# Sparse attention and two expert layers on one core: the first batch's attention in two halves of 288 tokens, and another order of the last products

## The chip, the cores and the metric

The kernel runs on one core of a Trainium2 chip. A core has five engines that run side by side, each through its own list of instructions in order: TensorE (PE) multiplies matrices, VectorE (DVE) and ScalarE (ACT) work on elements, GpSimd (POOL) too but without access to PSUM, and SyncE (SP) issues most of the DMAs, which move data between the core's memory (SBUF) and DRAM. TensorE writes to PSUM, eight banks of 128 x 512 floats. The metric is the device time of one execution in microseconds (us); lower is better.

## The reference

Two heads of 64 channels make a pair, four pairs a batch. Pairs 0 and 1 have the local mask, pairs 2 and 3 the strided one. The output of attention, 2304 tokens of 512 channels, goes through two expert layers.

```python
batch, n_heads, seq, head_dim = (4, 8, 576, 64)      # q, k, v
stride = 32
scores = scale * np.matmul(q, k.transpose(0, 1, 3, 2))
rel = pos[:, None] - pos[None, :]
mask_local = (rel >= 0) & (rel < stride)
mask_strided = (rel >= 0) & (pos[None, :] % stride == pos[:, None] % stride)
masks = [mask_local if h < H // 2 else mask_strided for h in range(H)]
attn = softmax(np.where(masks, scores, -1e9)) @ v
x = attn.transpose(0, 2, 1, 3).reshape(2304, 512)
h = x @ w_in                                         # 512 -> 2048
x = np.where(h >= 1, h, np.where(h <= -1, 0, (h + 1) ** 2 / 4)) @ w_out
r = np.maximum(x @ w2_in, 0)
out = (s * (r * r) + b) @ w2_out
```

## The kernel before, in words

**Tiling.** Tokens come in nine blocks of N = 256 for each expert layer: block g below 9 belongs to the first layer, g from 9 to 17 to the second. The 2048 inner channels make eight parts p of 256. `layer1(g, p)` gives the inner channels of a part for a block in 24 products of 128 x 256 into one PSUM tile h; `activate` applies the function and writes g; `layer2` multiplies by the second weights into y. Each float is held as the sum of two shorter numbers (names in h and l: xh, xl), so one product of the algorithm is three on TensorE. The second layer's second product is done by seven products m1 to m7 for four quadrants (Strassen's way in Winograd's form); `combine` makes the operands and `finish_fast` adds the seven into the quadrants c11, c12, c21, c22.

**Weights.** Each of 32 weight tiles of the first layer (wr{f}_{0 or 1}, 512 KB; 0 is w_in, 1 is w_out) is loaded and then converted: ScalarE makes c, VectorE makes wc in two instructions, ScalarE the high half of w, GpSimd the low half.

**Attention.** A `Unit` is one pair of one batch: loads of q, k, v; transposes on TensorE (t); scores (s); maximum, subtraction, exponential, sum, reciprocal and multiplication on VectorE and ScalarE; transposes of the result (p); products with v (o); copies into xr, from which `x_split` makes xh and xl of a block. In the strided pairs every 32nd token makes a group, 18 tokens by 3 residues in one tile of 54. The first batch's units borrow the memory of weight tiles 4 to 15 (`borrowed`), so those weights can only be loaded once the unit has read its data for the last time. Block 0 holds tokens 0 to 255, block 1 tokens 256 to 511.

**What sets the order.** `Order` records every instruction with a time at which it is due (`nc.now`, in slots of about 2.9 us, from the tables STARTS, PACE, W_TIMES and from the loops), and `Order.issue` then walks all engines with prices for every instruction and writes out the list of each engine. In front of the first product of layer 1 it also puts idle products (`fill`) into TensorE's list where it counts on a wait, to keep that engine's clock up. On the chip nothing of this is decided again: each engine takes its list in order. The passes begin with parts 0 and 1 of block 0, then parts 0 and 1 of block 1, and layer 2 follows two steps behind (LAG).

**Lines that matter here.** All instructions are written by one line, 383, so views are read by the names of tiles. The tables are STARTS (51), MEMORY (55), PASSES (62) and W_TIMES (73); the units are at 432, `x_split` at 790, `combine` at 873, `layer2_fast` at 895, `finish_fast` at 910. The call that plans the units:

```python
for i, t in enumerate(STARTS):
    b, pair = divmod(i, 4)
    plan(Unit(b, FIRST_PAIRS[pair], borrowed(MEMORY[i]) if i in MEMORY else main, i < QUICK, i < NATURAL), t)
```

Of the kernel before, what the change touches and what calls it, by code (L numbers as in the profile page):

```python
# [12 lines left out]
F32 = mybir.dt.float32  # L13
# [29 lines left out]
PITCH = 64  # L43
RES = 3
# [3 lines left out]
)  # L48
US_PER_SLOT = 2.9

STARTS = (-14, -11.2, -13.5, -11.7, 1.8, 8, 14.7, 21.4, 31, 37, 43, 48, 58, 64, 70, 76)
# [17 lines left out]

AGAIN = (6, *range(9, 16))  # L70


W_TIMES = {0: (-7, 1.9, 3), 1: (7.9, 1.9, 2.6)}
W_NEXT = {0: (113, 1.4), 1: (150, 3.2)}
W_AHEAD, W_RETRY, W_GAP = 3, 0.5, 1.2
# [18 lines left out]
N_CONST = N_MASK_L + N_MASK_S + P  # L94
# [7 lines left out]
def constants():  # L102

    row = np.arange(P)[:, None] % 64
    col = np.arange(64)[None, :]
    back = row % 32 - (col - 32)
    local = np.where((back >= 0) & (back < STRIDE), 0, DROP).astype(np.float32)
    last = np.where(row < 32, np.where(row >= col, 0, DROP), local).astype(np.float32)
    c = np.arange(54)[None, :]
    same = ((row // NPOS == c // NPOS) & (c % NPOS <= row % NPOS)) | (row >= 54)  # L110
    strided = np.where(same, 0, DROP).astype(np.float32)
    return np.ascontiguousarray(
        np.concatenate([last, local, strided, np.eye(P, dtype=np.float32)], axis=1)
    )


class Order:
# [151 lines left out]
    def issue(self):  # L269
# [40 lines left out]
        while done < n:  # L310
# [76 lines left out]
def attention_moe_moe(ctx, tc, q, k, v, w1_in, w1_out, w2_in, w2_out, s_in, b_in, consts, out):  # L387
# [7 lines left out]
    mask_l, mask_s, ident_b = narrow[:, :N_MASK_L], narrow[:, N_MASK_L:N_MASK_L + N_MASK_S], narrow[:, N_MASK_L + N_MASK_S:]  # L395
# [15 lines left out]
    filled = [0] * B  # L411
# [13 lines left out]
    def put(b, copy, o, i):  # L425
        copy(o, i)
        filled[b] += o.partition_size() * o.free_size()
# [232 lines left out]

    rooms, half_rooms, halves = [], [], {}
# [128 lines left out]
    def x_split(g):  # L790
# [57 lines left out]
    def activate(g, p, h):  # L848
        u = nc.tile(sb, [P, 2 * N], F32, tag="u", bufs=U_BUFS, name=f"u{g}_{p}")
        gt = nc.tile(sb, [P, 2, 2 * N], F32R, tag="g", bufs=3, name=f"g{g}_{p}")  # L850
# [22 lines left out]
    def combine(g, p, u, h, gt):  # L873
# [5 lines left out]
        gl = turn(1, (*main["raw"], main["s"]), f"gl{g}_{p}")[:, :7 * P].bitcast(F32R)  # L879

        def split(x, c):
            nc.scalar.activation(out=gh[:, c], in_=x, func=AF.Copy)
            nc.gpsimd.tensor_tensor(out=gl[:, c], in0=x, in1=gh[:, c].bitcast(F32), op=ALU.subtract)
# [6 lines left out]
        split(s4, slice(3 * P, 7 * P))  # L890
# [4 lines left out]
    def layer2_fast(g, p, p0, p1):  # L895
# [4 lines left out]
        left = dict(a11=0, a22=1, a12=2, s1=3, s2=4, s3=5, s4=6)  # L900
        for n, a, b in (
            (0, "a11", "b11"), (1, "a12", "b21"), (6, "a22", "t4"), (2, "s1", "t1"), (3, "s2", "t2"), (4, "s3", "t3"), (5, "s4", "b22"),
        ):
            c = slice(left[a] * P, (left[a] + 1) * P)
# [5 lines left out]
    def finish_fast(g, p0, p1):  # L910
# [3 lines left out]
        (c21, c22), (c11, c12), (m1, m2), (m5, m6), (m7, m3), (m4, _) = [(x[:, :HM], x[:, HM:]) for x in (*o, *y)]  # L914
# [67 lines left out]
    def borrowed(i):  # L982

        def piece(n, a=0, b=2 * DM):
# [7 lines left out]
            raw=[piece(0, 0, 768), piece(1, 0, 768)], qk=[piece(2), piece(3)], s=piece(4), p=[piece(5), piece(0, 0, 384)],  # L992
            v=[piece(6), piece(7)],
# [50 lines left out]
    with tc.manual_schedule():  # L1044
        nc.now = -100
        nc.sync.dma_start(out=ident, in_=consts[:, N_MASK_L + N_MASK_S:])
# [12 lines left out]
        for i, t in enumerate(STARTS):  # L1059
            b, pair = divmod(i, 4)  # L1060
            plan(Unit(b, FIRST_PAIRS[pair], borrowed(MEMORY[i]) if i in MEMORY else main, i < QUICK, i < NATURAL), t)
# [12 lines left out]
        for n, (g, p0, p1) in enumerate(PASSES):  # L1074
# [7 lines left out]
            nxt = PASSES[n + 1][0] if n + 1 < len(PASSES) else g  # L1082
            for i, (layer, b, *pp, p) in enumerate(order):
# [7 lines left out]
                if i == p1 - p0 + 1 and nxt not in xs:  # L1091
                    x_split(nxt)
                slot += 1
        for _, b, *pp, p in behind:
            nc.now += 1
            second(b, p, *pp)
# [27 lines left out]
```

## Time and profile before

| | |
|---|---|
| three runs | 897.02 us median, 896.44 to 901.4 |
| the profiled execution | 900.46 us, its span 898.7 us |
| TensorE | busy 878.2 us (98%), mean granted clock 0.988 |
| VectorE, ScalarE, GpSimd | busy 481.0, 491.7, 422.7 us |
| DMA | 103.38 MB, 125246 packets, 86656 of them under 512 B |

The span runs from the first to the last instruction that the profiler saw. A busy share says little of one stage, since the kernel has three: a start, in which attention of the first batch and the first weights come in; a long middle, in which the products follow each other; an end, in which the last products are added up and stored. The rows further down are read stage by stage.

### The profile page before, as it was taken

To read this page: it belongs to the slowest core of one execution; us is meant where nothing else is said; L and a number is where in the kernel's file an instruction comes from. 1 tells how busy PE (TensorE), PEld (TensorE's weight loads), DVE (VectorE), ACT (ScalarE), POOL (GpSimd) and SP (SyncE) were. 2 spreads that over 40 slices of the span, in tenths; PEclk is the share of its full clock that TensorE was granted. 3 is DMA by queue.
4 is the path that set the end of the run, shared out by engine and by line. 5 is a ranking of instruction groups with operands and counts; after the bars stand their busy time and mean duration, and the time that the engine had idled before them with its cause. 6 is when DMAs were issued, how large, how long until landed. Compare 5 with 4: busy or idle time off the path is not lost.

```text
span 898.7 us, 21961 instructions
## 1 busy us (share of the span) xinstructions
PE 878.2 (98%) x8872; PEld 866.4 (96%) x8872; DVE 481.0 (54%) x993; ACT 491.7 (55%) x1097; POOL 422.7 (47%) x362
## 2 busy tenths in 40 slices
PE   8889999999999999999999999999999999999996
PEld 7879999899999999999999999999999999999996
DVE  2598554444434342333685788545458954554455
ACT  2587685444534343333554587656667655555553
POOL 6186462112212212223464578777745765455544
PEclk9889999999999999999999999999999999999998
DMA  9998233322322221002635633426135332222211
GB/s 176 317 325 251 76 89 88 76 41 53 68 50 64 53 85 48 25 24 74 214 110 193 220 130 119 154 105 211 71 100 183 120 116 94 95 95 94 94 49 48
DMA packets 125246, 103.38 MB, mean 115 GB/s; under 512 B 86656, under 2 KB 103296, under 8 KB 125144
## 3 DMA queue, kind: packets, MB, share of 16 engines
q1 hardware_dynamic: 122008, 100.78, 37.5%
q8 instruction: 70, 1.15, 0.5%
q10 hardware_dynamic: 2368, 0.59, 0.4%
q0 software_dynamic: 768, 0.60, 0.4%
q14 instruction: 32, 0.26, 0.1%
HBM read 73.63 MB, written 28.31 MB: 113 GB/s over the span
## 4 chain that ended last, share of the span: by engine, by line
PE 95%; DVE 2%; issue 1%; DMA 1%; ACT 0%; SPq 0%; POOL 0%; DVEq 0%; ACTq 0%; POOLq 0%
PE h L383 45%; PE y L383 43%; PE s L383 3%; PE o L383 2%; PE idle L383 1%; DMA wr<-in_moe_w_in_dram 1%; PE t L383 1%; PE p L383 1%; DVE o L383 1%; DVE wc L383 0%; DVE u L383 0%; ACT u L383 0%; DVE h L383 0%; ACT h L383 0%; DVE qk L383 0%
## 5 line engine op out<-in xcount | busy, mean ns | idle before, releaser
L383 PE MATMUL h<-xh,w 128*128 128x256 f32 x2304 | 435.4, 281 | 3.9 <-ACT xr L383 2.0
L383 PEld LDWEIGHTS h<-xh,w 128*128 128x128 f32 x2304 | 364.3, 189 | 5.1 <-ACT xr L383 2.1
L383 PE MATMUL h<-xl,w 128*128 128x256 f32 x1152 | 323.6, 281 | 0.5 <-DVE xl L383 0.5
L383 PE MATMUL y<-g,w 128*128 128x256 f32 x1728 | 220.4, 281 | 0.0
L383 PEld LDWEIGHTS h<-xl,w 128*128 128x128 f32 x1152 | 218.0, 189 | 1.0 <-DVE xl L383 0.8
L383 POOL TENSOR_TENSOR g<-u,g 128x512 fp32r<-128x512 f32 x72 | 95.6, 1327 | 246.7 <-ACT g L383 166.7
L383 PEld LDWEIGHTS y<-g,w 128*128 128x128 f32 x1728 | 209.0, 188 | 0.8
L383 PE MATMUL y<-w,g 128*128 128x256 f32 x864 | 158.7, 281 | 0.9 <-DVE o L383 0.9
L383 ACT ACTIVATE u<-h 128x512 f32<-128x512 f32 x144 | 85.9, 598 | 117.6 <-DVE h L383 55.8
L383 PEld LDWEIGHTS y<-w,g 128*128 128x128 f32 x864 | 132.9, 188 | 1.3 <-DVE o L383 1.3
L383 DVE TENSOR_SCALAR u<-h 128x512 f32<-128x512 f32 x72 | 49.6, 688 | 142.5 <-PE h L383 139.9
L383 PE MATMUL y<-w,gl 128*128 128x256 f32 x432 | 121.0, 282 | 0.0
L383 POOL TENSOR_TENSOR gl<-u,g 128x384 fp32r<-128x384 f32 x72 | 76.1, 1057 | 95.4 <-ACT g L383 93.5
L383 ACT ACTIVATE u<-u,half 128x512 f32<-128x512 f32 x72 | 51.9, 722 | 113.7 <-DVE u L383 113.6
L383 POOL TENSOR_TENSOR gl<-s,g 128x512 fp32r<-128x512 f32 x72 | 97.8, 1358 | 33.1 <-ACT g L383 31.2
L383 ACT ACTIVATE g<-u 128x512 fp32r<-128x512 f32 (+1 forms) x144 | 83.1, 577 | 32.1 <-DVE u L383 25.2
L383 DVE TENSOR_SCALAR h<-h,sbt 128x512 f32<-128x512 f32 x72 | 58.7, 816 | 68.1 <-ACT h L383 67.9
L383 POOL TENSOR_TENSOR w<-wc,w 128x512 fp32r<-128x512 f32 x56 | 76.6, 1375 | 37.9 <-ACT w L383 36.0
L383 PEld LDWEIGHTS y<-w,gl 128*128 128x128 f32 x432 | 80.9, 188 | 0.0
L383 DVE TENSOR_TENSOR o<-y,o 128x256 f32<-128x256 f32 x120 | 46.7, 417 | 45.3 <-PE y L383 45.1
L383 DVE TENSOR_TENSOR u<-h,u 128x512 f32<-128x512 f32 x72 | 49.5, 687 | 26.3 <-ACT u L383 25.9
L383 DVE TENSOR_SCALAR wc<-wr 128x512 int32<-128x512 int32 x64 | 45.4, 722 | 19.8 <-DMA wr<-in_moe_w_in_dram 10.6
(91 smaller groups left out, 934.5 us busy)
## 6 DMA issues: line engine op xcount, KB each, us to landing
wr<-in_moe_w_in_dram SPq DMA_DIRECT2D x32, 512.0 KB
wr<-in_moe_w_out_dram SPq DMA_DIRECT2D x32, 512.0 KB
x<-o SPq DMA_DIRECT2D x36, 256.0 KB
scratch<-x SPq DMA_DIRECT2D x18, 512.0 KB
y<-o SPq DMA_DIRECT2D x22, 256.0 KB
scratch<-y SPq DMA_DIRECT2D x11, 512.0 KB
out_dram<-o SPq DMA_DIRECT2D x18, 256.0 KB
xhd<-xh SPq DMA_DIRECT2D x8, 512.0 KB
```

The lines of the kernel that those rows point to most:

```text
L383: getattr(getattr(self.nc, engine), op)(*args, **kw)
```

## The change

Two parts, and new numbers in the tables.

1. **The first batch's units come in halves** (`Half`): tokens 0 to 287, then 288 to 575. The first halves of all four pairs stand in front of the second halves. A half loads 288 rows of q and k (the local pairs also only half of v), transposes them in one bank, has one tile of scores instead of two, and its own softmax, p, o and copies. A second half of a strided pair looks at the keys of both halves. Its k transposes and all copies of the strided pairs into xr go to VectorE instead of ScalarE. Block 0 may be split once the first halves are there.
2. **The last block's end** (`last_two`; the seven products also stand in another order, PRODUCTS, in all blocks of the second layer): the last two parts are multiplied product by product, both parts of m1, m6, m2, m5, then of m4, m7, then m3; the sums of the four quadrants are made as the products come, with GpSimd and ScalarE taking some of them; every quadrant has a DMA of its own, two on SyncE's queue and two on ScalarE's. `layer1` of the last part moves in front of the second product of the part two before, and the low half of the last two parts' s goes from GpSimd to VectorE.

```diff
+PRODUCTS = ((0, "b11"), (4, "t2"), (2, "b21"), (3, "t1"), (1, "t4"), (5, "t3"), (6, "b22"))
+HALF_PACE = (
+    (0, ("load_qk", 0)), (0, ("load_qk", 1)), (1, ("load_v",)), (3, ("trans", 0)), (3.1, ("trans", 1)), (3.6, ("scores",)),
...
-STARTS = (-14, -11.2, -13.5, -11.7, 1.8, 8, 14.7, 21.4, 31, 37, 43, 48, 58, 64, 70, 76)
+HALF_STARTS = ((-14.0, -9.0), (-13.0, -8.0), (-14.0, -8.43), (-13.5, -8.28))
+STARTS = (1.07, 7.73, 14.33, 22.7, 31, 37, 43, 48, 58, 64, 70, 76)
-W_TIMES = {0: (-7, 1.9, 3), 1: (7.9, 1.9, 2.6)}
-W_AHEAD, W_RETRY, W_GAP = 3, 0.5, 1.2
+W_TIMES = {0: (-7.02, 1.9, 3.0), 1: (8.01, 1.9, 2.6)}
+W_AHEAD = 4.25
...
-                dma = max(dma, t + 1.0) + o.nbytes() / run * (10 + 0.039 * run) / 16e3
+                dma = max(dma, t + 1.0) + o.nbytes() / run * (15 + 0.04 * run) / 16e3
...
+    class Half(Unit):
+        def __init__(self, b, pair, mem, h):
+            self.nb, self.kw = (6, 27 * (h + 1)) if self.strided else (5, 64)
...
+        def load_qk(self, w):
+            queue = nc.scalar if w and not self.h else nc.sync
+            for a in range(2):
+                queue.dma_start(
+                    out=t[:, :, 64 * a:64 * a + 64],
+                    in_=self.heads((q, k)[w])[a][HALF * self.h:HALF * (self.h + 1)].rearrange("(i s) d -> s i d", s=96),
+                )
+        def trans(self, w):
+            bk = bank(f"t{w}_{self.id}")[:, :HALF]
...
+            copy = nc.vector.tensor_copy if h and w else act_copy
...
+        def scores(self):
+            self.sp = bank(f"s_{self.id}")[:, :nb * kw]
...
+        def smul(self):
+            nc.vector.tensor_tensor(out=self.s, in0=self.s, in1=self.by(self.mx), op=ALU.mult)
...
+        def evac_o(self, copy):
+            if self.strided:
+                for g in range(2):
...
+                    put(self.b, nc.vector.tensor_copy, o, self.ob[g][:, :135].rearrange("p (m e t) -> p m e t", e=RES, t=NPH), h)
+                put(self.b, nc.vector.tensor_copy, t[:, 30:], self.ob[0][:, 135:153].rearrange("p (e t) -> p e t", t=NPH), h)
...
-                assert filled[b] == P * NC * S, (g, filled)
+                assert filled[b] == P * NC * S or hi <= HALF and ready[0] == P * NC * HALF, (g, filled)
...
-        split(s4, slice(3 * P, 7 * P))
+        split(s4, slice(3 * P, 7 * P), nc.vector if g == LAST[0] and p >= NP - 2 else nc.gpsimd)
...
+    def last_two(g, p0, part):
...
+        for i, n in ((0, 0), (0, 1), (0, 2), (0, 3), (1, 0), (1, 1), (1, 2), (1, 3), (0, 4), (0, 5), (1, 4), (1, 5), (0, 6), (1, 6)):
+            multiply(n, *pairs[i])
+        nc.scalar.activation(out=c11, in_=m1, func=AF.Copy)
+        nc.gpsimd.tensor_tensor(out=p11, in0=c11, in1=p11, **add)
+        nc.vector.tensor_tensor(out=c21, in0=m6, in1=c11, **add)
+        nc.gpsimd.tensor_tensor(out=p21, in0=c21, in1=p21, **add)
+        nc.vector.tensor_tensor(out=c22, in0=m5, in1=c21, **add)
+        nc.gpsimd.tensor_tensor(out=p22, in0=c22, in1=p22, **add)
+        nc.vector.tensor_tensor(out=c11, in0=m2, in1=p11, **add)
+        leave(1, 0, c11, nc.sync)
+        nc.vector.tensor_tensor(out=p12, in0=c22, in1=p12, **add)
+        nc.scalar.activation(out=p11, in_=m7, func=AF.Copy)
+        nc.vector.tensor_tensor(out=p21, in0=m7, in1=p21, **add)
+        nc.gpsimd.tensor_tensor(out=c22, in0=p11, in1=p22, **add)
+        leave(0, 1, c22, nc.sync)
+        nc.vector.tensor_tensor(out=c21, in0=p21, in1=m4, op=ALU.subtract)
+        leave(0, 0, c21, nc.scalar)
+        nc.vector.tensor_tensor(out=c12, in0=m3, in1=p12, **add)
+        leave(1, 1, c12, nc.scalar)
...
-        for i, t in enumerate(STARTS):
+        for i, (t0, t1) in enumerate(HALF_STARTS):
+            mem = borrowed(MEMORY[i]) if i in MEMORY else rest
+            for h, t in enumerate((t0, t1)):
+                u = Half(0, FIRST_PAIRS[i], mem, h)
+                u.clear()
+                plan(u, t)
+        for i, t in enumerate(STARTS, 4):
...
+            if n + 1 == len(PASSES):
+                order.insert(-2, order.pop(-2))
```

What that makes of the lists is shown at three places.

SyncE's queue around the first weights (mem and raw are a unit's q, k and v, named by the borrowed weight; wr0_f_x is weight tile f, x of the first layer). Before:

```order
L383 DMA mem4_0_214<-in_v_dram 128x4x64 x2
L383 DMA mem4_0_214<-in_v_dram 64x64
L383 DMA mem4_1_261<-in_v_dram 128x4x64 x2
L383 DMA mem4_1_261<-in_v_dram 64x64
L383 DMA wr0_0_0_305<-in_moe_w_in_dram 128x4x256
L383 DMA wr0_1_0_324<-in_moe_w_in_dram 128x4x256
L383 DMA wr0_0_1_351<-in_moe_w_out_dram 128x1024
L383 DMA wr0_2_0_384<-in_moe_w_in_dram 128x4x256
```

and now:

```order
L401 DMA mem4_0_136<-in_v_dram 128x2x64 x2
L401 DMA mem4_1_145<-in_v_dram 128x2x64 x2
L401 DMA raw0_0_3_161<-in_q_dram 96x3x64 x2
L401 DMA mem11_0_175<-in_q_dram 96x3x64 x2
L401 DMA wr0_0_0_200<-in_moe_w_in_dram 128x4x256
L401 DMA wr0_1_0_212<-in_moe_w_in_dram 128x4x256
L401 DMA mem15_0_84<-in_q_dram 96x3x64 x2
L401 DMA mem15_1_69<-in_k_dram 96x3x64 x2
L401 DMA mem12_0_113<-in_v_dram 128x2x64 x2
L401 DMA mem12_0_113<-in_v_dram 64x64
```

The first two weights now stand behind the loads of the first halves (16 DMAs on this queue) instead of behind all 24 of the batch; 28 of the 44 loads that there are now follow them. The third weight, wr0_0_1, stands between second halves.

TensorE around the first product of layer 1 (h0_0; o are the products with v, p the transposes in front of them, idle the products that fill). Before:

```order
L383 MATMUL o0_0_1_558<-mem7_0_99,mem4_0_214 64x32 x2
L383 MATMUL o0_0_1_558<-mem7_0_99,mem4_1_261 64x32 x2
L383 MATMUL p0_0_3_608<-ident_65,s_0_3_71 128x128 x4
L383 MATMUL idle_83<-u_67 128x256 x29
L383 MATMUL h0_0_673<-xh0_648,w0_0_0_657 128x256
L383 MATMUL h0_0_673<-xl0_661,w0_0_0_657 128x256
L383 MATMUL p0_0_2_684<-ident_65,mem9_0_73 128x128 x4
L383 MATMUL p1_0_3_691<-ident_65,s_0_3_71 128x128 x2
```

and now:

```order
L401 MATMUL o0_0_1a_447<-mem5_1_414,mem4_0_136 64x32
L401 MATMUL o0_0_1a_447<-mem5_1_414,mem4_1_145 64x32
L401 MATMUL idle_78<-u_67 128x256 x12
L401 MATMUL p_0_3a_499<-ident_65,s0_0_3_96 128x128 x3
L401 MATMUL idle_78<-u_67 128x256 x11
L401 MATMUL h0_0_530<-xh0_516,w0_0_0_505 128x256
L401 MATMUL o0_0_3a_535<-early_528,v0_0_3_106 64x27
L401 MATMUL o1_0_3a_537<-early_528,v0_0_3_106 64x27
```

The idle products stay, 23 here in two groups instead of 29 in one. Behind the first product stand instructions of both halves: five more products of h0_0 are spread over the next 42 rows of the list, and its other 18, all of h0_1's and those of h1_0 follow p_0_1b and p_0_3b, the transposes of two second halves, at row 173 and 174.

VectorE's last rows (y15_4_0 to 3 are the banks of the seven products, o the quadrants, scratch the partial sum of the earlier parts). Before:

```order
L383 TENSOR_TENSOR o15_4_0_12187<-y15_4_1_12053,o15_4_1_12176 128x256
L383 TENSOR_TENSOR o15_4_1_12176<-y15_4_0_12033,o15_4_1_12176 128x256
L383 TENSOR_TENSOR o15_4_1_12176<-y15_4_1_12053,o15_4_0_12187 128x256
L383 TENSOR_TENSOR o15_4_0_12187<-y15_4_2_12062,o15_4_0_12187 128x256
L383 TENSOR_TENSOR o15_4_1_12176<-y15_4_2_12062,o15_4_1_12176 128x256
L383 TENSOR_TENSOR o15_4_0_12187<-y15_4_1_12053,o15_4_0_12187 128x256
L383 TENSOR_TENSOR o15_4_0_12187<-o15_4_0_12187,y15_4_3_12047 128x256
L383 TENSOR_TENSOR o15_4_0_12187<-o15_4_0_12187,scratch_4754 128x512
```

and now:

```order
L401 TENSOR_TENSOR gl15_6_12270<-s15_6_12252,g15_6_12259 128x512
L401 TENSOR_TENSOR s15_7_12286<-h15_7_12195,s15_7_12286 128x128
L401 TENSOR_TENSOR last_l_12303<-s15_7_12286,last_h_12293 128x512
L401 TENSOR_TENSOR o15_4_0_12334<-y15_4_0_12231,o15_4_1_12326 128x256
L401 TENSOR_TENSOR o15_4_0_12334<-y15_4_1_12237,o15_4_0_12334 128x256
L401 TENSOR_TENSOR o15_4_1_12326<-y15_4_1_12237,scratch_4915 128x256
L401 TENSOR_TENSOR scratch_4915<-o15_4_0_12334,scratch_4915 128x256
L401 TENSOR_TENSOR scratch_4915<-y15_4_2_12241,scratch_4915 128x256
L401 TENSOR_TENSOR o15_4_1_12326<-y15_4_3_12263,scratch_4915 128x256
L401 TENSOR_TENSOR o15_4_0_12334<-scratch_4915,y15_4_2_12241 128x256
```

The wide addition of the partial sum, 128x512, is gone from the last place; the partial sum is added quadrant by quadrant on the way, and the row that reads the last product's bank, y15_4_3, is the last but one.

## Rows read from the trace of the kernel before

**Rows 1.** Windows: busy time by engine in each stretch, TensorE clock, DMA share, GB/s.

```profile
0.00:60.00 60.00, 49.18 (x714) 45.96 (x715) 32.16 (x63) 32.28 (x71) 30.29 (x41) 0.86 1.09 260
21.00:51.80 30.80, 25.32 (x407) 23.48 (x402) 19.45 (x36) 18.43 (x43) 9.43 (x7) 0.81 1.03 298
60.00:150.00 90.00, 90.00 (x1113) 87.81 (x1112) 56.17 (x97) 63.27 (x170) 51.62 (x42) 1.00 0.49 145
890.00:899.00 9.00, 1.78 (x15) 1.54 (x13) 3.82 (x8) 0.39 (x1) 1.78 (x2) 0.70 0.15 58
```

**Rows 2.** Timeline of TensorE, 30 to 64: start, length, instruction, count, idle before.

```profile
32.92 0.66 PE L383 MATMUL o<-mem,mem 64*64 64x32 f32 x30 [2.95 <-issue]
...
35.57 5.81 PE L383 MATMUL idle<-u 128*128 128x256 f32 x29
41.22 0.28 PE L383 MATMUL h<-xh,w 128*128 128x256 f32 x1
...
47.56 0.58 PE L383 MATMUL h<-xh,w 128*128 128x256 f32 x1 [2.03 <-ACT xr L383]
...
58.16 0.36 PE L383 MATMUL h<-xh,w 128*128 128x256 f32 x1 [1.62 <-DVE u L383]
...
61.07 3.00 PE L383 MATMUL y<-g,w 128*128 128x256 f32 x24
```

**Rows 3.** Timeline of SyncE's DMA queue, 0 to 30: start, time of issue, count.

```profile
1.65 2.37 SPq L383 DMA_DIRECT2D mem<-in_q_dram  x4
...
13.17 10.34 SPq L383 DMA_DIRECT2D mem<-in_v_dram  x12
23.56 1.14 SPq L383 DMA_DIRECT2D wr<-in_moe_w_in_dram  x2
```

**Rows 4.** DMA view, packets of 15 to 27, then of 27 to 31.

```profile
DMA packets 6579, 2.16 MB, mean 180 GB/s; under 512 B 6019, under 2 KB 6485, under 8 KB 6578
...
DMA packets 1132, 1.53 MB, mean 382 GB/s; under 512 B 44, under 2 KB 1001, under 8 KB 1131
```

**Rows 5.** Timelines of ScalarE, GpSimd and VectorE, 42 to 52.

```profile
42.09 0.60 ACT L383 ACTIVATE mem<-p 128x512 f32<-128x512 f32 x1 [2.27 <-PE p L383]
...
43.83 3.94 POOL L383 TENSOR_TENSOR w<-wc,w 128x512 fp32r<-128x512 f32 x3 [4.16 <-ACT w L383]
...
45.15 2.90 DVE L383 TENSOR_SCALAR wc<-wr 128x512 int32<-128x512 int32 x2 [4.21 <-DMA wr<-in_moe_w_in_dram]
...
49.41 2.36 DVE L383 TENSOR_TENSOR xl<-xr,xh 128x512 fp32r<-128x512 f32 x2
```

**Rows 6.** Groups of VectorE by form: busy, mean ns of one, idle before.

```profile
L383 DVE TENSOR_SCALAR wc<-wr 128x512 int32<-128x512 int32 x64 | 45.4, 722 | 19.8 <-DMA wr<-in_moe_w_in_dram 10.6 <-DMA wr<-in_moe_w_out_dram 4.9 <-POOL w L383 4.2
L383 DVE SCALAR_TENSOR_TENSOR wc<-c,wc 128x512 int32<-128x512 int32 x64 | 42.9, 680 | 6.9 <-ACT c L383 6.3
...
L383 DVE COPY o<-y 128x512 f32<-128x512 f32 x18 | 12.4, 688 | 4.6 <-PE y L383 4.2
...
L383 DVE TENSOR_REDUCE mx<-s 128x6 f32<-128x324 f32 x8 | 4.0, 496 | 11.6 <-PE s L383 11.3
```

**Rows 7.** The end: chain of waits, then timelines of TensorE, VectorE, SyncE's queue.

```profile
884.18 7.14 PE y L383 x59
...
891.50 0.28 PE L383 MATMUL y<-w,gl 128*128 128x256 f32 x1
...
891.40 2.41 DVE L383 TENSOR_TENSOR o<-y,o 128x256 f32<-128x256 f32 x6 [2.92 <-PE y L383]
...
894.30 1.12 DVE L383 TENSOR_TENSOR o<-o,scratch 128x512 f32<-128x512 f32 x1
...
894.90 0.88 SPq L383 DMA_DIRECT2D out_dram<-o  x2
```

**Rows 8.** Timelines of VectorE at 879 and of GpSimd at 889.

```profile
879.62 1.57 DVE L383 TENSOR_TENSOR o<-o,scratch 128x512 f32<-128x512 f32 x1
...
889.23 1.28 POOL L383 TENSOR_TENSOR gl<-s,g 128x512 fp32r<-128x512 f32 x1
```

More of the change, by code (lines that the diff above doesn't have):

```diff
@@ L111, in constants @@
     strided = np.where(same, 0, DROP).astype(np.float32)
+    at, pos = np.divmod(row % 32, NPH)
+    halves = []
+    for h in range(2):
+        n = NPH * (h + 1)
+        c = np.arange(3 * n)[None, :]
+        halves.append(np.where((at == c // n) & (c % n <= pos + NPH * h) | (at >= 3), 0, DROP).astype(np.float32))
     return np.ascontiguousarray(
-        np.concatenate([last, local, strided, np.eye(P, dtype=np.float32)], axis=1)
+        np.concatenate([last, local, strided, *halves, np.eye(P, dtype=np.float32)], axis=1)
     )
@@ L423, in x_raw, with put @@
         return xr[b]
-    def put(b, copy, o, i):
+    def put(b, copy, o, i, h=None):
         copy(o, i)
-        filled[b] += o.partition_size() * o.free_size()
+        n = o.partition_size() * o.free_size()
+        filled[b] += n
+        if h is not None:
+            ready[h] += n
     def act_copy(o, i):
@@ L849, in activate @@
         u = nc.tile(sb, [P, 2 * N], F32, tag="u", bufs=U_BUFS, name=f"u{g}_{p}")
-        gt = nc.tile(sb, [P, 2, 2 * N], F32R, tag="g", bufs=3, name=f"g{g}_{p}")
+        if (g, p) == LAST:
+            gt, _ = xs[g, 1] = [nc.tile(sb, [P, NC, N], F32R, tag=f"x{i}", bufs=2, name=f"last_{i}") for i in "hl"]
+        else:
+            gt = nc.tile(sb, [P, 2, 2 * N], F32R, tag="g", bufs=3, name=f"g{g}_{p}")
         if g >= NBLK:
@@ L935, in finish_fast, with last_part, multiply, leave @@
             nc.sync.dma_start(out=sums[g][:, i] if p1 < NP else out[r0:r0 + P, :], in_=o[i])
+    def last_part(g, p0):
+        part = piece(f"part{g}_{p0}").rearrange("p c n -> p (c n)").rearrange("p (i d) -> p i d", d=DM)
+        nc.sync.dma_start(out=part, in_=sums[g])
+        return part
+    def last_two(g, p0, part):
+        y, o = ys.pop(g), [turn(2, (main["qk"][1], main["v"][1]), f"o{g}_{p0}_{i}")[:, :DM] for i in range(2)]
+        (c21, c22), (c11, c12), (p21, p22), (p11, p12), (m1, m6), (m2, m5), (m4, m7), (m3, _) = [
+            (x[:, :HM], x[:, HM:]) for x in (*o, part[:, 0], part[:, 1], *y)
+        ]
+        pairs = [(p, gs.pop((g, p))) for p in (NP - 2, NP - 1)]
+        def multiply(n, p, x):
+            a, b = PRODUCTS[n]
+            o, c, w = y[n // 2][:, n % 2 * HM:(n % 2 + 1) * HM], slice(a * P, a * P + P), wt[1, p][b]
+            for i, j in ((0, 0), (0, 1), (1, 0)):
+                nc.tensor.matmul(o, x[i][:, c], w[:, j], start=False, stop=p == NP - 1 and i == 1, skip_group_check=True)
+        def leave(i, j, c, queue):
+            r0 = (g - NBLK) * N + i * P
+            queue.dma_start(out=out[r0:r0 + P, j * HM:(j + 1) * HM], in_=c)
+        nc.in_line = True
+        for i, n in ((0, 0), (0, 1), (0, 2), (0, 3), (1, 0), (1, 1), (1, 2), (1, 3), (0, 4), (0, 5), (1, 4), (1, 5), (0, 6), (1, 6)):
+            multiply(n, *pairs[i])
+        nc.in_line = False
+        add = dict(op=ALU.add)
+        nc.scalar.activation(out=c11, in_=m1, func=AF.Copy)
[15 more added lines that the diff above has]
+        leave(1, 1, c12, nc.scalar)
@@ L1092, in attention_moe_moe @@
                     x_split(nxt)
+                elif i == p1 - p0 + 1 and n + 1 == len(PASSES):
+                    part = last_part(g, p0)
                 slot += 1
-        for _, b, *pp, p in behind:
-            nc.now += 1
-            second(b, p, *pp)
+        nc.now += 1
+        last_two(g, p0, part)
         nc.issue()
```

203 lines of the change are left out of this document (186 added, 17 removed).

## The prediction

> **What bounds the kernel now.** I read the windows first [rows 1]. From 60 to 150 us TensorE is busy 90.00 of 90.00 us at clock 1.00, so in the middle an engine that gets faster gives nothing. What can be won lies at two ends: in the first 60 us TensorE is busy 49.2 us at clock 0.86, with many idle products among it, and from 890 on it is busy 1.78 of 9 us. The reader is to see that a microsecond by which the steady stretch begins earlier is a microsecond off the end, if the other engines keep up.
>
> Then the timeline of TensorE in the start [rows 2]. The marker that I use is the first product of layer 2, at 61.07: behind it there is no gap for 89 us. In front of it the rows show 2.95 us of waiting that no engine explains, 29 idle products for 5.81 us, a first product of layer 1 at 41.22, another at 47.56 behind ScalarE's copies into xr, and the first of block 1 (h1_0) at 58.16, behind VectorE.
>
> Then the loads. SyncE issues the batch's 24 loads first, and the first weight only at 23.56 [rows 3]. The data come at a mean of 180 GB/s from 15 to 27 us, when they are short rows of q, k and v, and at 382 GB/s from 27 to 31, when they are weights [rows 4]. So weights have been there since about 28 us, and still nothing flows: ScalarE waits until 42.09 for TensorE's p, which stands behind those 29 idle products; GpSimd waits for ScalarE until 43.83; VectorE's wait of 4.21 us up to 45.15 is put down to a weight DMA, but it ends when GpSimd's first w of that row is done and its buffer is free [rows 5]. The start is bound by a chain through all lists, after the data have come. VectorE's last xl ends at 51.77 (49.41 + 2.36).
>
> **The change part by part: the start.** Bytes in front of the first weight, from the shapes: constants 0.26 MB, first halves of q and k 0.59 each, local v 0.52, strided v 0.59 (GpSimd loads it whole): 2.56 MB, at 180 GB/s 14.2 us, from about 1.5 us on. The first weight lands near 17 us instead of near 28, the second at 18. The other halves (1.77 MB, 9.8 us) and the third weight land by 29; from the fourth weight on nothing comes earlier than before, the sum of bytes being the same. SyncE issues 44 loads instead of 24. I cost that at nothing, hidden by the bytes: four loads took 2.37 us when the queue was empty, 0.59 each, so 44 take 26 us of the 31 until the fourth weight. If issuing were the bound, at the 0.86 us that each of the 12 loads of v took, it would be 17 us later; but those twelve carry 1.1 MB and ran at the bytes' pace.
>
> The first product of layer 1 can then start near 24 us (weight at 17, four instructions of conversion behind other work, and GpSimd's loads until about 22), but only six products of h0_0 do; the other 18 stand behind second halves. What sets the marker is VectorE's list. From the first copy of a strided first half into xr to xl of block 1 it has 53 instructions: 6 of the TENSOR_SCALAR kind at 0.72 us, 5 SCALAR_TENSOR_TENSOR at 0.68, and 42 smaller ones on 5 to 512 elements. By the copy of 512 at 0.69 and the reduction of 324 at 0.50 [rows 6] these cost 0.15 us plus about 1.05 ns an element: 8 copies of 135 2.3, 4 of 18 0.7, 4 of 288 1.8, 16 reductions, subtractions and multiplications of about 320 7.8, two xl 1.4, eight small 1.4, together 15.4. With 4.3 and 3.4 that is 23.1, and less 53 times 0.07, by which each starts before the former ends, 19.4 us. They start at about 26, when the first strided o is done. Without any wait they end at 45.4. Before, from 21.0 to 51.8, VectorE worked 19.45 us of 30.8, 63% [rows 1]: at that share they end at 56.8. I take 51, the middle: the second halves' data are there by 29, so the waits for data fall away, but the waits for TensorE and ScalarE in the lists' order stay. h1_0 follows after the low half of the fourth w_in tile and 12 products of h0_1 (GpSimd about 1.3, 12 times 0.12): 53.7 instead of 58.16, **4.5 us earlier**. By the two bounds it is 10 us earlier or 1.3 later.
>
> Against this: when h1_0 starts, seven weight tiles are converted, before ten. Three tiles are 3 x (0.72 + 0.68) = 4.2 us of VectorE. Its share in the steady stretch is 56.2 of 90 [rows 1], so of the 8.4 us until the first of these tiles is wanted (h1_0, a product of layer 2, h1_1) it can use some 3.2 to catch up: **1.0 us lost**, between 0 and 4.2. Splitting also adds some 90 small products to attention, each two records of 0.022 us (30 in 0.66) [rows 2]: 4 us of TensorE, which the idle products and waits of the start hide; uncovered, all 4. Start: 3.5 us won.
>
> **The end.** The last product ends at 891.78 (891.50 + 0.28) and the span at 898.7: 6.9 us. In between stand additions of 256 in a row of six, and one of 512 until 895.42 with the partial sum, and 3.28 us of storing [rows 7]. After: GpSimd's chain of four quadrant additions, each half of its 1.28 us [rows 8], begins when m1 is done, six products (2.1 us) before the end, and ends some 1.1 us behind the last product; VectorE's two last additions end at about 1.0. With 3.28 us of storing that is 4.4 instead of 6.9: 2.5 won. If storing half the bytes is quicker or VectorE decides alone, up to 3.2; if the four stores queue, 1.0. A wait could come in front: the last part's low halves are wanted 6.7 us after h ends (two steps of 21 products and 15 more, 0.117 us each). Before, from the last h at 884.18 to the end of that split, 890.51, it took 6.33 [rows 7, 8]; now both parts' chains share ScalarE within 2.8 us, while the split itself moves to VectorE. I take 0.2. End: **2.3 us won**.
>
> [...] In the trace VectorE's addition of 512 with both inputs in SBUF took 1.57 us at 879.62, beside GpSimd's, and 1.12 at 894.30 [rows 7, 8]. [...] The split that moves to VectorE is such an instruction.
>
> The other edits cost nothing: the order of the seven products is the same work, the wait for the partial sum is long over, the first memsets of GpSimd (under 2 us) only delay loads of v that queue anyway.
>
> **Sum.** 898.7 - 3.5 - 2.3 = 892.9 of span, 894.7 on the profiled execution's 900.46. The median of the runs, 897.02, lies 3.4 lower, and the prediction is made on it: 897.0 - 5.8 = **891.2**.
>
> **The rivals.** *Nothing comes of the halves.* The lists put 18 of h0_0's 24 products and all of block 1 behind the second halves, so starting early may only stretch the start. For it: [rows 5], a wait that moves through the lists; against it, that 5.81 us of idle products stood on that chain. Start 0, end 2.3: 894.7.
>
> *VectorE runs nearly without waits.* For it: once its wait had ended, two of its rows alone fill 5.3 of the 6.6 us from 45.15 to xl [rows 5]; against it, 63%. The marker then hangs on the fourth w_in tile, 8 us won: 886.7.
>
> [...]
>
> *The lists lock.* On the other side: VectorE's copies of k and of the strided o wait for small products, these for VectorE's multiplications of other units, and its conversions stand behind. At a share of 50% xl of block 1 ends at 26 + 19.4 / 0.5 = 64.8, h1_0 at 67.5, 9.3 later than before; with 1.0 lost and 2.3 won: 905.0. From a share of about 55% down the kernel is slower than before by what can be told.
>
> **Chances.** A difference of 0.5%, 4.5 us, is about what a measurement of this kernel can tell from none. My forecast 0.37 (its own range 889 to 893.5), nothing from the halves 0.24, VectorE dense 0.20, the end waits 0.08, the lists lock 0.11. Faster means below 892.5: most of the forecast's share, all of the dense case, a little of two others, together 0.60. Same 0.29, slower 0.11. The range leaves out most of the lock and reaches to the dense case with a longer end: 884.5 to 897.
>
> **What would show it.** The first weight issued near 10 us; a first product of layer 1 at 22 to 26; xl of block 1 ending at 51; h1_0 near 54 and the first product of layer 2 near 56.5 without a gap of over 2 us in the 15 us behind it; the last product 4.4 us before the end of the span, with no wait of TensorE in front of it. It is wrong if the marker is not earlier than 60, if VectorE's share from 26 to its xl is under 0.6, or if the end still takes over 6 us.

## The result: slower, by 0.8%

The changed kernel takes 905.15 us (median of 10 runs, 901.71 to 909.74), the kernel before beside it 897.88 (10 runs, 896.44 to 901.4): a ratio of 1.0083, 95% interval 1.0065 to 1.010. The forecast was 891.2, and the range ended at 897.0. The profiled execution took 903.00 with a span of 901.2, where before had 900.46 and 898.7. These two are single executions out of runs that spread over 5 and 8 us, and differ by 2.5 us where the medians differ by 7.3. So I take from them where time went, and the sizes of the parts from runs against runs.

The windows of the profile after (columns as in [rows 1]: the stretch and its length; busy us and count of TensorE, its weight loads, VectorE, ScalarE and GpSimd; granted clock, DMA share, GB/s):

```profile
0.00:60.00 60.00, 53.00 (x976) 48.19 (x977) 34.77 (x87) 28.95 (x71) 30.48 (x47) 0.91 0.88 215
28.95:56.35 27.40, 25.01 (x495) 21.49 (x499) 20.90 (x54) 16.48 (x38) 9.12 (x7) 0.88 0.84 248
60.00:150.00 90.00, 88.26 (x1024) 85.88 (x1023) 61.60 (x101) 68.06 (x187) 51.67 (x42) 1.00 0.62 179
890.00:901.20 11.20, 7.08 (x61) 6.88 (x59) 4.99 (x14) 2.85 (x6) 4.73 (x6) 0.96 0.14 47
```

Against [rows 1], TensorE works more in the first 60 us (53.00 for 49.18, 976 products for 714), and is no longer without a gap behind them (88.26 of 90). The second row is the stretch from VectorE's first strided copy to xl of block 1: 20.90 us of work in 27.40, 76%.

The timeline of TensorE after, for [rows 2]:

```profile
23.50 2.51 PE L401 MATMUL idle<-u 128*128 128x256 f32 x11 [3.10 <-issue]
25.81 0.83 PE L401 MATMUL p_3a<-ident,s 128*128 128x128 f32 x3
26.30 1.64 PE L401 MATMUL idle<-u 128*128 128x256 f32 x11
27.78 0.28 PE L401 MATMUL h<-xh,w 128*128 128x256 f32 x1
...
57.61 0.39 PE L401 MATMUL h<-xh,w 128*128 128x256 f32 x1 [0.19 <-DVE u L401]
...
60.59 3.00 PE L401 MATMUL y<-g,w 128*128 128x256 f32 x24
```

The first product of layer 1 comes at 27.78 (before 41.22), but h1_0 at 57.61 (58.16) and the first product of layer 2 at 60.59 (61.07): of 13 us in front, half a microsecond is left at the marker, and some 2 us of the second batch's attention (t x12, s x72), of which only five t stood in front of it before. Even that half is the chance of one execution. The marker in a run with the old start and in one with the halves, which are told of below (b_best, a_best):

```profile
57.62 2.89 PE L392 MATMUL y<-g,w 128*128 128x256 f32 x24
```

```profile
60.03 2.88 PE L410 MATMUL y<-g,w 128*128 128x256 f32 x24
```

In five other traces with the old start it lies at 55.7 to 57.6 (b_place, b_best, b_zero, b_32, b_end), in three others with the halves at 59.2 to 60.1 (a_place, a_best, a_oldend). The 61.07 from which the prediction set out is the latest of its kind, by 3.4 us. By the other traces the marker comes 2 to 3 us later with the halves, some 2 of them by the attention that moved in front of it.

SyncE's queue after, for [rows 3]:

```profile
12.98 1.03 SPq L401 DMA_DIRECT2D wr<-in_moe_w_in_dram  x2
...
16.25 6.27 SPq L401 DMA_DIRECT2D mem<-in_v_dram  x6
...
26.74 0.47 SPq L401 DMA_DIRECT2D wr<-in_moe_w_out_dram  x1
27.25 3.14 SPq L401 DMA_DIRECT2D mem<-in_v_dram  x6
30.43 3.24 SPq L401 DMA_DIRECT2D mem<-in_q_dram  x2
...
34.73 1.49 SPq L401 DMA_DIRECT2D wr<-in_moe_w_in_dram  x1
```

and the packets that all queues moved from 20 to 37 us, in the DMA view of the kernel before and then of the changed one:

```profile
DMA packets 6058, 5.13 MB, mean 302 GB/s; under 512 B 3370, under 2 KB 5523, under 8 KB 6056
```

```profile
DMA packets 6466, 2.13 MB, mean 125 GB/s; under 512 B 6302, under 2 KB 6315, under 8 KB 6463
```

The first weight is issued at 12.98 instead of 23.56, the fourth only at 34.73, where before had issued it at 25.28. From 20 to 37 us the queues move 3 MB less than before. The windows of the six loads of v at 16.25 and of the 16 DMAs behind them:

```profile
16.25:22.50 6.25, 4.15 (x176) 3.66 (x175) 4.74 (x13) 4.60 (x15) 2.65 (x4) 1.00 1.11 221
22.56:30.99 8.43, 7.03 (x88) 6.63 (x88) 2.71 (x7) 2.04 (x5) 1.75 (x3) 0.80 0.69 162
```

The last but one number is the DMA share: in the first stretch the DMA engines are full, in the second they are not.

The end, for [rows 7]: TensorE's, VectorE's and ScalarE's queue's timelines after.

```profile
896.81 0.28 PE L401 MATMUL y<-w,last_l 128*128 128x256 f32 x1
...
897.57 0.41 DVE L401 TENSOR_TENSOR o<-scratch,y 128x256 f32<-128x256 f32 x1
...
897.69 0.86 ACTq L401 DMA_DIRECT2D out_dram<-o  x2
```

From the end of the last product, 897.09, to the end of the span, 901.18, it takes 4.1 us instead of 6.9; 4.4 was predicted. But this last product is 5.3 us later than before.

All of TensorE's time in the two profiled executions, summed from the timelines (a product counts from its start to the start of the next, less gaps of over 0.1 us):

| us | before | after | difference |
|---|---|---|---|
| idle products | 18.9 | 16.1 | -2.7 |
| gaps until 100 us | 9.5 | 5.8 | -3.7 |
| attention (t, s, p, o) | 62.1 | 66.3 | +4.2 |
| layer 1 (h), 3456 products | 411.4 | 417.4 | +6.0 |
| layer 2 (y), 3240 products, the last left out | 385.6 | 386.5 | +0.9 |
| gaps later | 2.7 | 3.4 | +0.7 |
| behind the last product | 6.9 | 4.1 | -2.8 |

The largest term is one that nobody touched: the same 3456 products of layer 1. The chain of waits shows them in rows of 24 (start, length), before and then after, near 300 us, where TensorE is busy all the time at clock 1.00 in both:

```profile
306.17 2.80 PE h L383 x24
...
327.04 2.83 PE h L383 x24
```

```profile
305.90 2.80 PE h L401 x24
...
326.84 2.88 PE h L401 x24
...
368.18 2.87 PE h L401 x24
```

Some rows are as before, 2.80 to 2.84, and others 2.87 or 2.88: 120 ns a product. The granted clock, 1.00 from 300 to 400 us in both, does not tell them apart.

### The profile page after: what moved, and what is told of

It is laid out like the page before. It is cut to its first block, busy times and chain, and to the rows that moved or that the text cites. A ratio compares the mean times of both kernels' runs of the same rounds, so it can differ in the third digit from the quotient of the medians.

```text
span 901.2 us, 22398 instructions
## 1 busy us (share of the span) xinstructions
PE 886.5 (98%) x9048; PEld 872.8 (97%) x9048; DVE 489.2 (54%) x1022; ACT 492.2 (55%) x1098; POOL 424.3 (47%) x369
## 4 chain that ended last, share of the span: by engine, by line
PE 91%; DMA 3%; issue 2%; SPq 1%; DVE 1%; ACT 1%; POOL 0%; DVEq 0%; POOLq 0%; ACTq 0%
PE h L401 45%; PE y L401 42%; PE s L401 2%; DMA wr<-in_moe_w_out_dram 1%; PE o L401 1%; SPq L401 1%; DMA mem<-in_q_dram 1%; PE p L401 1%; PE t L401 0%; POOL w L401 0%; DMA mem<-in_k_dram 0%; DVE o L401 0%; DVE wc L401 0%; DVE u L401 0%; DVE s L401 0%
## 5 line engine op out<-in xcount | busy, mean ns | idle before, releaser
L401 PE MATMUL h<-xh,w 128*128 128x256 f32 x2304 | 441.6, 283 | 1.6 <-DVE s L401 1.4
L401 PE MATMUL y<-w,g 128*128 128x256 f32 x852 | 154.9, 281 | 0.0
L401 PEld LDWEIGHTS y<-w,g 128*128 128x128 f32 x852 | 130.3, 188 | 0.1
L401 PE MATMUL y<-w,gl 128*128 128x256 f32 x426 | 118.1, 281 | 0.0
L401 POOL TENSOR_TENSOR gl<-s,g 128x512 fp32r<-128x512 f32 x70 | 92.1, 1316 | 31.4 <-ACT g L401 28.4
L401 POOL TENSOR_TENSOR w<-wc,w 128x512 fp32r<-128x512 f32 x56 | 74.6, 1339 | 53.9 <-ACT w L401 53.6
L401 ACT ACTIVATE g<-u 128x512 fp32r<-128x512 f32 (+1 forms) x143 | 82.7, 578 | 30.1 <-DVE u L401 23.6
L401 ACT ACTIVATE g<-s 128x512 fp32r<-128x512 f32 x71 | 44.6, 628 | 23.3 <-DVE s L401 23.2
```

Of the source, the lines that this page charges most:

```text
L401: getattr(getattr(self.nc, engine), op)(*args, **kw)
```

## The experiments

**Where the operands lie.** Both kernels' products on 256 columns are in the same order in program and trace, one to one (6800 and 6796), so each product of the trace has the SBUF addresses of its two operands. The program places buffers in the order of their first use. The change makes the table of masks `narrow` wider (81 columns, from 620 to 782 bytes a partition) and alters that order, so everything behind lies elsewhere. Taken modulo 128 bytes, with the mean distance from one product's start to the next from 80 to 880 us (distances over 150 ns left out):

| | x at, weights at | ns a product (products) |
|---|---|---|
| layer 1, before | 64, 32 | 117.1 (3035) |
| | 64, 0 | 115.5 (214) |
| layer 1, after | 64, 64 | 119.4 (2187) |
| | 64, 32 | 117.0 (935) |
| | 64, 0 | 117.5 (95) |

Inside one execution of the changed kernel there are two paces in its two large groups, and one is that of before. The first four runs move buffers and nothing else; instructions and order stay. Gaps are unused tiles:

```diff
+PADS = {"w4_0": 24, "xh": 8, "w9_1": 24}      # a_place; b_place: {"w11_0": 8, "xh": 24, "g": 8}
 ...
+            if tag in PADS:
+                pool.tile([P, PADS[tag]], F32, tag=f"pad_{tag}", bufs=1, name=f"pad_{tag}")
             self.tiles[x.tensor.name] = pool.tile(shape, dtype, tag=tag, bufs=bufs, name=name)
```

and for a_best and b_best the small tiles first, then the operands other than weights, the weights last (a number in the list is a gap, in floats of 4 bytes):

```diff
+LAYOUT = ['half', 'sbt', 'narrow', 8, 'mx', 'sm', 16, 'raw0', 'raw1', 'as', 'xh', 'xl', 'g', 16]
 ...
+        for at, tag in enumerate(LAYOUT):
+            if isinstance(tag, int):
+                pool.tile([P, tag], F32, tag=f"gap{at}", bufs=1, name=f"gap{at}")
```

(b_best has 16 for the 8, its table being narrower.) a_place:

> The changed kernel with three gaps of 96, 32 and 96 bytes in SBUF and nothing else: the instructions and their order are the same. With them the weights lie at addresses of 32 modulo 128 (as in the kernel before), x at 64 and g at 64, where the changed kernel has most weights at 64, x at 64 and g at 96. Theory P (the address of the two operands sets TensorE's pace): in the trace of the changed kernel a product of layer 1 takes 119.4 ns where both operands lie at 64, and 117.0 where the weights lie at 32, and the kernel before has 117.1 at 64 and 32. So some 2300 products get 2.4 ns quicker, 5.5 us: about 899.5 on a median of 905.15, a ratio to before of 1.002. Theory L (the order of the lists, the start above all, costs the time): no change, 905, ratio 1.008. Theory C (the pace is that of the chip or the execution): no change either, and products of 119 ns in this trace too.

Measured: 901.99, ratio 1.0041 (1.0020 to 1.0062). Layer 1 went from 118.7 ns in the mean to 117.5. That is 3.2 of the 5.5 us that P promised; before had 117.0.

> The kernel before with gaps of 32, 96 and 32 bytes, so that most weights and x lie at 64 modulo 128 and g at 96, as in the changed kernel; nothing else is changed. Theory P: layer 1's products go from 117.1 to some 119.4 ns where both lie at 64, about 2300 of 3456: 5.5 us slower, 903.4, ratio 1.006. Theories L and C: 898, ratio 1.000.

Measured: 903.93, ratio 1.0058 (1.0039 to 1.0077). P holds, L and C fall: the old kernel, with all its lists, is slowed by moving its buffers. Layer 1 took 118.5 ns at 64 and 64, 118.2 over all of it.

> The changed kernel with its buffers placed on purpose: all weights at 0 modulo 128, x, g and the low halves of g at 64. Theory P, by the groups of products in the two traces (64 against 0: 115.5 ns for 214 products before, 117.6 for 96 after; 64 against 32: 117.0): layer 1 gains 2 to 4 ns on some 2300 products and 0 to 1.5 on the rest, 5 to 10 us: 895 to 900, ratio 0.997 to 1.002. Theories L and C: 905.

Measured: 881.96, ratio 0.9813 (0.9778 to 0.9848), far below what was expected: layer 1 114.9 ns, layer 2 113.6 in the first expert layer (g streams against weights) and 115.9 in the second (seven products, weights stream against g). The small groups with a distance of 64 in the first traces had understated it: 115.5 ns before, 117.5 after, and 117.3 in b_place. So the distance of a product's own operands does not set its pace alone, where the products around it lie otherwise; why, no run shows.

> The kernel before with the same placing on purpose (weights at 0, x, g and its low halves at 64 modulo 128), its lists unchanged. Theory P: layer 1 at 115.5 to 117 instead of 117.1 and layer 2 some 1 ns quicker, 0.5 to 9 us: 889 to 897, ratio 0.990 to 0.999. Theories L and C: 898, ratio 1.000.

Measured: 883.47, ratio 0.9829 (0.9792 to 0.9866): 15 us off the old kernel without touching an instruction, and again below what was expected.

Is it the distance between the two operands, or the address of each? b_zero leaves out the gaps of b_best in front of the operands, b_32 makes them 32 bytes:

> The kernel before with weights, x, g and the low halves of g all at addresses of 0 modulo 128 in SBUF; nothing else is changed. Theory R (what counts is how the two operands of a product lie to each other: 64 apart is quick, the same address modulo 128 is slow): products of layer 1 at 118 to 120 ns, as with 64 and 64 in the changed kernel, and layer 2 the same: 898 to 908, ratio 1.000 to 1.011. Theory A (each operand by itself has to lie at a multiple of 64, and what was slow is an address of 32): 113.5 to 116 ns as in the kernel placed on purpose, 883, ratio 0.983.

> The kernel before with weights at 0 and x, g and the low halves of g at 32 modulo 128; nothing else is changed. Theory R in its strict form (only the same address modulo 128 collides, all other distances are quick): as at 64, 113 to 115.5 ns and 883, ratio 0.983. Theory R in steps (the nearer, the slower): 117, as where x lay at 64 and the weights at 32 in the kernel before: 896, ratio 0.997. Theory A (an address of 32 is slow by itself) also 117.

Measured: b_zero 914.19, ratio 1.0182 (1.0157 to 1.0208); b_32 902.85, ratio 1.0047 (1.0028 to 1.0066). Both are slower than any theory had put them; their order is that of R in steps. Rows of 24 in the chain of waits of b_best, b_32 and b_zero:

```profile
320.61 2.72 PE h L392 x24
323.33 2.72 PE y L392 x24
```

```profile
310.85 2.82 PE h L392 x24
```

```profile
307.14 2.88 PE h L392 x24
310.02 2.88 PE y L392 x24
```

| ns a product, by distance modulo 128 | layer 1 | layer 2, g and weights | layer 2, combined weights and g |
|---|---|---|---|
| 64 (b_best) | 115.2 | 114.4 | 115.8 |
| 32 (b_32) | 117.8 | 117.7 | 119.7 |
| 0 (b_zero) | 119.9 | 119.9 | 120.0 |

Theory A falls: 0 and 0 is the slowest. R holds in steps, for kernels in which all operands lie alike: the quickest rows have 113 ns (2.72 for 24), and the same address costs 6% of it. That 64 and 64 is nearly as slow in the changed kernel as 0 and 0 here (119.4 and 119.9), and 64 and 32 in the kernel before about as 32 and 0 here (117.1 and 117.8), speaks for the distance and against either address alone. b_zero and b_best have the same lists and differ by 31 us.

**The change by itself, in one placing.** With weights at 0 and the rest at 64 the two parts of the change can be told apart:

```diff
 b_end:    the kernel before, with last_two, PRODUCTS and LAST of the change
 a_oldend: the changed kernel without last_two and LAST; PRODUCTS stays
+        for _, b, *pp, p in behind:
+            nc.now += 1
+            second(b, p, *pp)
-        nc.now += 1
-        last_two(g, p0, part)
```

PRODUCTS gives the seven products other banks; outside the last two parts they are still multiplied in the order of before.

> The kernel before with the start of before and the end of the changed kernel (the last two parts by products and quadrants, and the new order of the seven products in all parts of layer 2), weights at 0 and the other operands at 64 modulo 128. Against the kernel before in the same placing (883.5, ratio 0.983). Theory: the end gives what its trace shows, 4.1 instead of 6.8 us behind the last product: 880.8, ratio 0.980. Rival: what the end saves comes back as a wait in front of it (splits in one line): 883, ratio 0.983.

> The changed kernel with the halves of the first batch and the old end, in the same placing (the whole change in it: 882.0, ratio 0.981; the kernel before in it: 883.5, 0.983). Theory H (the halves win on idle products and waits of the start what they lose on 180 more small products of TensorE, 3.8 us): 883 to 885, ratio 0.983 to 0.985. Rival (the halves win 3.5 as was predicted): 880, ratio 0.979.

| us (ratio) | old end | new end |
|---|---|---|
| old start | 883.47 (0.9829) | 880.57 (0.9804, 0.9782 to 0.9825) |
| halves | 886.45 (0.9870, 0.9846 to 0.9893), old end with the new banks | 881.96 (0.9813) |

From b_best to b_end the new end saves 2.9 us, as its theory said; b_end's trace has 4.0 us behind the last product where b_best has 6.8. The 4.5 of the lower row is no clean measure: a_oldend keeps the new banks, and its old end takes 7.6 us behind the last product, 0.8 more than in b_best. So the halves cost 1.4 by the right column, and the 3.0 of the left one hold these 0.8. Neither part is clear of the intervals (2 to 3 us to either side of each run) by its clean pair; the two pairs of each part agree in sign. What is shown is that the halves do not win the 3.5 us that were predicted. The whole change in one placing, a_best against b_best, is 1.5 us quicker, inside the intervals: with the operands placed alike, no slowdown is seen.

**The start.** Timelines of ScalarE, VectorE and GpSimd after, 19 to 29 us:

```profile
26.68 0.49 ACT L401 ACTIVATE early<-p_3a 128x384 f32<-128x384 f32 x1 [4.91 <-PE p_3a L401]
...
19.39 0.16 DVE L401 TENSOR_SCALAR sm_3a<-sm_3a 128x6 f32<-128x6 f32 x1
...
21.38 1.24 DVE L401 TENSOR_SCALAR sm_2a<-sm_2a 128x6 f32<-128x6 f32 x1
...
27.73 0.69 DVE L401 SCALAR_TENSOR_TENSOR wc<-c,wc 128x512 int32<-128x512 int32 x1 [3.73 <-ACT c L401]
...
21.33 1.26 POOL L401 TENSOR_TENSOR w<-wc,w 128x512 fp32r<-128x512 f32 x1 [3.60 <-ACT w L401]
```

The data of p_3a are ready at 20.7, when VectorE has multiplied s. TensorE has twelve idle products in front of it, and 3.10 us of waiting inside them. Behind p_3a stand ScalarE's `early`, c, VectorE's wc, GpSimd's w. Two runs tested that, in the placing of a_best:

```diff
+        del fillers[KEPT:]          # a_fewidle: KEPT = 76, the last 23 idle products left out
```
```diff
+        last = max(start[i] for i, o in enumerate(self.ops) if ... == "p_0_3a")      # a_p3first
+        fillers[76:88] = [last + 1e-6] * 12
+        del fillers[64:70]
```

> The changed kernel in the same placing without the last 23 idle products of the start, those between the first local outputs and the first product of layer 1, which stand in front of the transposes of unit 3 (the data of these are there at 20.8 us, and they run at 25.9). Theory F (these idle products are on the chain that sets the start): the first product of layer 1 at 24 instead of 28.3, the first of layer 2 at 57 instead of 60, 879, ratio 0.978. Rival W (the second halves' data and the lists set the start anyway): the first product of layer 1 earlier, the first of layer 2 at 59 to 60, 881 to 882, ratio 0.981. Rival K (the clock falls for longer without them): 883 to 886.

Measured: 881.12, ratio 0.9820 (0.9795 to 0.9846): no gain, as W said. Its timeline and its window of 20 to 40 us, in the slowest of its five executions (885.30):

```profile
24.68 0.36 PE L412 MATMUL h<-xh,w 128*128 128x256 f32 x1
25.50 1.66 PE L412 MATMUL o_3a<-early,v 54*64 54x27 f32 x44 [0.46 <-ACT early L412]
```

```profile
20.00:40.00 20.00, 15.38 (x263) 12.75 (x257) 10.39 (x28) 6.80 (x19) 3.76 (x3) 0.66 0.70 165
```

The first product comes at 24.68, as F said, but then TensorE runs at a mean clock of 0.66 where a_best has 0.91; the 44 products of o_3a take 1.66 us instead of 0.90. In this execution the first product of layer 2 is at 64.2. In this trace what leaving out the idle products gains in the list is lost again in the clock (K); the median shows neither a gain nor a loss.

> The changed kernel, weights at 0 and the other operands at 64, with the transposes of unit 3's first half (p_3a) in front of the twelve idle products that stood ahead of them, and six idle products of the row of 30 left out, so that p_3a is also in front of TensorE's 3 us of waiting at 20.4. Theory F (p_3a at 25.8 instead of 20.8 is on the chain of the start, by ScalarE's early, its c, VectorE's wc, GpSimd's w): the first product of layer 1 at about 25 instead of 28.3, the first of layer 2 at 57 to 58 instead of 60, 879, ratio 0.978. Rival W (the start hangs on the second halves and VectorE's list behind them): first product earlier, the first of layer 2 at 59.5 to 60, 882, ratio 0.981.

Measured: 880.48, ratio 0.9799 (0.9772 to 0.9825); first product of layer 1 at 26.94, of layer 2 at 59.17. That is 1.5 us less than a_best, inside the intervals, and 0.9 us at the marker, between what F and W said: most of the start hangs on something else. With b_end it is the fastest run here.

```diff
-            queue = nc.scalar if w and not self.h else nc.sync
+            queue = nc.scalar if w and (self.strided or not self.h) else nc.sync
```

> The changed kernel in the same placing, with the second halves of k of the strided units on ScalarE's DMA queue instead of SyncE's: four loads fewer for SyncE in front of the fourth weight. Theory S (SyncE's issue, about 0.5 us a load, holds the weights back: 101 to 190 GB/s from 20 to 37 us, where before had 326 to 376 GB/s from 25 to 40): the fourth weight is issued 2 us earlier and the first product of layer 2 comes 1 to 2 us earlier, 880 to 881, ratio 0.980. Rival W (VectorE's list is the bound): no change, 882, ratio 0.981.

Measured: 889.54, ratio 0.9906 (0.9877 to 0.9936), a miss: neither theory had it. ScalarE's queue and ScalarE, then TensorE, in its timeline:

```profile
9.20 1.77 ACTq L410 DMA_DIRECT2D mem<-in_k_dram  x2
11.00 1.28 ACT L410 ACT_TABLE_LOAD   x1 [11.00 <-DMA raw<-in_k_dram]
...
13.36 0.94 PE L410 MATMUL s_0a<-mem,mem 64*32 64x64 f32 x34 [3.05 <-ACT mem L410]
```

The four loads hold ScalarE's own list until 11.0 (after: 6.29), so its copies of t come 4.7 us late and everything behind them. SyncE issued the fourth weight at 33.62, in a_best at 33.63: not earlier at all. Whether SyncE's issue is on the path of the start stays open: this run moved the load to a worse place.

## Why the prediction was wrong, step by step

**The step that failed** is the one that cost nothing and was not argued: "a microsecond by which the steady stretch begins earlier is a microsecond off the end, if the other engines keep up". It took the 830 us behind the marker as given. From the first product of layer 2 to the last product it was 830.4 us before and 836.2 after: the products of both layers took 6.9 us more and gaps 0.9 more, attention 2.1 less. The products themselves got slower, 117.0 to 118.7 ns in layer 1, because weights and g moved by 32 bytes. b_place shows that on the old lists (+0.58%, 5.2 us), a_place on the new (-0.4%). Over the runs the parts come to 5.2 for the placing, 1.7 for the half nanosecond by which layer 1 is slower yet in the changed kernel than in b_place (118.7 and 118.2, 3456 products, from single executions), 1.4 for the halves and -2.9 for the end, the clean pair of each: 5.4 of 7.3 us. The rest is within the intervals. No view of the profile before shows an address; but rows of 24 under one clock differed there too, 2.80 to 2.84, and I had read only the shares of busy time, which are 100% either way.

**The start: 3.5 us predicted, nothing won.** The marker was to come at 56.5; it came at 60.59, and "not earlier than 60" was one of my own signs of being wrong. For xl I took 51. VectorE's stretch began 3 us late (28.95 instead of 26) and ended at 56.35. The share was about the one assumed (76%; 19.4 of 25 is 78%), the work 20.9 instead of 19.4; the rest is the late start: 3.10 us of TensorE's waiting at 20.4 and idle products in front of p_3a, so the weights' conversion stopped for 3.73 us. I had put the first product at 24; it came at 27.78. And the 4.5 us were counted from a start that was itself late (61.07, where other executions have 55.7 to 57.6): I had moved the sum to the median of the runs, but not the start.

"I cost that at nothing, hidden by the bytes", of SyncE's 44 loads, was wrong for the later ones. The six loads of v at 16.25 take 6.27 us, 1.04 each, but at the pace of full DMA engines (share 1.11). From 22.56 to 30.99 SyncE issues without a pause, 0.53 us a DMA, and the share is 0.69: there the bytes hide nothing. Then it waits 2.3 us until the third weight has landed. "From the fourth weight on nothing comes earlier than before" was worse than that: it came 9.4 us later. The 47 loads in front of it took 0.70 us each (1.67 to 34.73), between the 0.59 of my sum and the 0.86 that I dismissed. What this costs at the marker no run isolated.

The 90 small products, which idle products and waits were to hide: there are 180 more records, as counted, the attention takes 4.2 us more, and they are not hidden. Idle products and gaps fell by 6.4 us, but the new products took two thirds of that. And the profiled execution of before had the longest start of its kind: over five traces with the old start (before, b_place, b_best, b_zero, b_end) idle products and gaps until 100 us are 25.7 in the mean, over four with the halves (after, a_place, a_best, a_oldend) 23.6: 2.1 won, and 3.3 lost on the products of attention (61.8 and 65.1 in the mean). So for the start the rival "Nothing comes of the halves" was the right one, and 0.24 too little for it, though its time, 894.7, failed by the same step as mine; the lock of the lists (905.0, near the time measured) did not happen: its signs, a share of 50% and h1_0 at 67.5, are not in the trace. That it came nearest is luck.

**The end: 2.3 us predicted, 2.9 measured** (b_best to b_end), 2.8 in the trace. The sum of its parts held: 4.1 us behind the last product for 4.4. No wait came in front of it: TensorE is busy 7.08 of the 7.09 us from 890 to the end of its last product, so the case in which the end waits, with 0.08, did not come.

On VectorE's work beside GpSimd's [rows 7, 8]: in the trace of before both additions of 512 stand beside one of GpSimd's (879.33 to 880.63 and 893.62 to 894.88) and end 0.56 and 0.54 us behind it, after 1.57 and 1.12 us. In the changed kernel VectorE's split beside GpSimd's took 0.68 us at 891.22, with no lengthening of its own (0.69 at 892.80, beside none); they met for 0.4 us, and GpSimd's, the later one, took 1.26 at 891.53 where one of its kind took 1.02 at 889.43. In the start VectorE's instruction on 6 elements takes 1.24 us beside GpSimd's 1.26 (rows above; 0.16 alone, at 19.39), and they end within 0.03 us; here it stands beside a wait that is longer anyway. In these four pairs it is the later one that took long; what holds it, the traces don't show.

**My own chances.** 0.11 for slower was too low, not since a lock was likely but since nothing in the sum stood for what a change does to code that it doesn't touch.

## What to carry to other kernels

When every product of a TensorE-bound kernel gets slower or faster by one or two per cent after an edit elsewhere, compare rows of equal work under the same clock first, then the addresses of the two operands. Place stationary and moving operands 64 bytes apart modulo 128 on purpose, before tuning lists: here it was worth 15 us, five times the best part of the change. (Only streams of products on 256 columns with weights loaded for each were tried, and the distances 0, 32 and 64.) And compare two versions of a list only in one placing, or the placing is what is measured.

## What the runs showed of the hardware

In this kernel TensorE's pace hangs on where its two operands lie in SBUF: in the means of b_best, b_32 and b_zero a product on 256 columns takes 114.4 to 115.8 ns at a distance of 64 bytes modulo 128 (113 in the quickest rows), 117.7 to 119.7 at 32, 119.9 to 120.0 at 0, at a granted clock of 1.00 from 300 to 400 us in all three. The addresses of both operands together change the time of a product by up to 6% (113 to 120.0 ns). Why their distance counts, the runs don't show.

TensorE's longest waits put down to "issue" come at fixed places of its instruction list: in front of its 450th and 962nd instruction (products, weight loads and waits for semaphores) in the kernel before, 2.27 and 2.95 us, and of its 706th and 962nd in the changed kernel, 3.10 and 0.59 us: multiples of 256 apart. They go with the list and not with the time: the 30 products o behind the 2.95 us start at 32.92 in before, and in b_end, behind 2.34 us, at 29.00. The wait in the changed kernel from 20.4 to 23.5 has one packet of the queue named `instruction` in it, among 1060 of data (DMA view, 20.5 to 23.5 us):

```profile
q1 hardware_dynamic: 1060, 0.25, 55.7%
q0 software_dynamic: 41, 0.02, 5.2%
q8 instruction: 1, 0.02, 2.9%
```

The wait of 2.95 us in before (29.97 to 32.92) has one such packet too; in the other two, from 14.77 to 17.04 there and from 32.94 to 33.53 in the changed kernel, none begins. What the waits are for, no run tested; the places, 256 apart, and the lengths are what the traces show.
